# A chunked recurrence whose inputs come from the host with channels on the rows

## The chip, the cores and the metric

The kernel runs on one core of a Trainium2 chip. The metric is the device time of one execution in microseconds (us), the median of several runs. Five engines work side by side: TensorE (PE; PEld is its weight load), VectorE (DVE), ScalarE (ACT), GpSimd (POOL) and SyncE (SP, which here issues the DMAs). Each engine takes its own instructions strictly in order.

## The reference, cut to what matters

```python
def _attn_ref(r, k, v, w, a, b):                 # each (4, 8, 768, 40): batch, head, step, channel
    state = zeros((B, H, D, D))
    for t in range(S):
        y[:, :, t] = einsum('bhd,bhde->bhe', rt, state)
        Sa = einsum('bhde,bhe->bhd', state, at)
        state = state * wt[:, :, None, :] - einsum('bhd,bhe->bhde', Sa, bt) + einsum('bhd,bhe->bhde', vt, kt)
    return y

def reference(...):
    x = _attn_ref(r, k, v, w, a, b)              # then (4, 768, 320)
    x = _moe_ref(x, w_gate, wq, wk, wv, wo)      # causal attention of 4 experts, the best 2 per row weighted
    return _moe2_ref(x, w_in, w_spatial, b_spatial, w_out)   # relu(x w_in), norm, mixing over steps, w_out
```

The change touches only the inputs of `_attn_ref`; the two later stages are as they were.

## The kernel before, in words

The 768 steps of a batch are cut into chunks of C = 64. Inside a chunk the recurrence is solved as a triangular system, so that only one state of 40x40 per head goes from chunk to chunk. Two batches go together, and three chunks of both make a **unit**: 8 units in all (2 pairs of batches, 4 stretches of 192 steps). A unit has its 8 heads as 4 pairs, and a pair's 2x40 channels lie on 104 rows (40, a gap to row 64, 40).

**First phase** of a unit (`p1`), which needs no state. Per pair: `p_w` brings w with channels on the rows and makes running products forward (PP, L159) and back (RPE, L162 and L165); `p_kb` multiplies b and k by RPE (L171), `p_a` multiplies a by PP (ABD, L178) and sends it to WL by DMA (L180); `p_t` makes the products of kb with ABD on PE (L189), masked by DVE into WL (L193) and copied by ACT into the tiles TD and T21 (L196, L197); `p_kbt` transposes kb (L206, L207). Then, per unit: `p_l` transposes TD into L (L217, copy L218), `p_sub` inverts the 32-row triangles by 62 DVE instructions of which each needs the one before it (L227 and L229 in turn), and `p_xt` transposes the inverse (L237, copies L241).

The inputs lie in memory with steps as rows, so w, b, k and a of each pair come in as a slab of 96-step blocks (four DMAs of 30 KB, L134, six slab buffers) and are turned by four PE transposes (`tr`, L141) into a PSUM tile. b, k and a are read there by DVE; w is copied by ACT into W first (L157).

**Second phase** (`p2`, once per chunk, both batches in turn): `f_w` (L370, ACT copy L374), `f_st` (L380, L383), `amat(0)` (L316), `f_u1` (L387, L391, L393), `amat(1)` (L316, mask L322), `f_t21` (L397, L400), `ys` (L333), `f_u2` (L404, L407), `rr` (r transposed, L295, copy L296), `yk` (L341, L344, stored), `f_s` (new state, L416, then SV by DVE, L419 and L420) and `vt` (the solved rows and v of the chunk transposed together, L302, copy L304). `f_w` of the next chunk needs SV. `amat`, `ys` and `yk` belong to the chunk before.

**What sets the order.** PE's order is written out by hand: each chunk calls `pump` five times, and `pump` puts pieces of the first phase of later units there, by a list of (time, piece): the pairs' pieces of unit i + 2 over the 15 pumps of unit i, and `p_l`, `p_sub` and `p_xt` of unit i + 1 in the same unit i. So while unit 2 runs, DVE inverts the triangles of unit 3 and the pairs of unit 4 are made ready. Before unit 0 the whole first phase of unit 0 and the pairs of unit 1 run alone. The order on DVE, ACT, POOL and SP is fixed when the program is built, by the scheduler's own estimate of times.

Of the kernel before, what the change touches and what calls it, by code (L numbers as in the profile page):

```python
# [54 lines left out]

def recurrence(ctx, tc, r, k, v, w, a, b, ident, store_x, pre=None, tail=None):
    nc = tc.nc
    B, H, S, D = r.shape
    C = 64
# [29 lines left out]

    SLAB = [ap.tile([TS, SL, 2, 64], F32, name=f"slab{n}") for n in range(NSL)]  # L90
    RR = cp.tile([128, H, 64], F32, name="RR")
    WL = [home(i, 3).tile([128, H, UT], F32, name=f"WL{i}") for i in range(3)]
# [21 lines left out]
    nc.vector.memset(scan1[:, :, 0:1], 1.0)  # L114
    for t in SLAB:
        nc.vector.memset(t[:, :, :, D:], 1.0)
    nc.vector.memset(RR[:, :, D:], 1.0)
    for t in W65:
        nc.vector.memset(t, 0.0)
    for t in WL + VU + sum(SV, []):  # L120
        nc.gpsimd.memset(t, 0.0)

    src = {"w": w, "k": k, "b": b, "a": a}
    uses = []

    def load(n):
        if n >= len(uses):
            return
        nm, i, p = uses[n]
        bb, u = units[i]  # L130
        for q in range(BQ):
            for z in range(SL // BQ):
                t0 = u * CQ * C + z * TS
# [3 lines left out]
    def tr(nm, i, p):  # L137
        n = uses.index((nm, i, p))
        pt = ps.tile([128, SL, TS], F32, name="p1", bufs=P1B)
# [3 lines left out]
        return pt[:Q].rearrange("e s p -> e (s p)")  # L143

    def ct(x):
        return x.rearrange("e (c t) -> e c t", c=UC)

    def p1(i):
# [3 lines left out]
        def p_w(p):  # L152
            n = i * NP + p
            w65, rpe = W65[n % 2], RPE[n % 2]
# [76 lines left out]
        def p_xt(t0):  # L231
# [7 lines left out]
            for g in range(2):  # L239
# [10 lines left out]
        def spread(lst, g0, g1):  # L250
# [12 lines left out]

    def load_step(dst, of, g, q):
        if g >= nst:
            return
        i, c = divmod(g, CQ)
        bb, u = units[i]
        t0 = (u * CQ + c) * C
        nc.sync.dma_start(dst[:, :, :D], of[bb * BQ + q, :, t0:t0 + C, :].rearrange("h t d -> t h d"))  # L270

    def load_sv(g):
        for q in range(BQ):
            load_step(SV[q][g % 2][64:], v, g, q)

    def load_vu(g):
        for q in range(BQ):
            load_step(VU[q][64:], v, g, q)

    def load_r(g):  # L280
        for q in range(BQ):
            load_step(RR[64 * q:64 * q + 64], r, g, q)

    def y_items(g):
# [3 lines left out]
        s0 = [S0[q][g % 2] for q in range(BQ)]  # L288
        rt = [RT[g % RTB][:, :, q * C:(q + 1) * C] for q in range(BQ)]
        st = {}  # L290

        def rr():
            pr = ps.tile([128, NP, BQ * C], F32, name="p1", bufs=P1B)
# [3 lines left out]
            load_r(g + 1)  # L297

        def vt(q):
            pv = ps.tile([128, NP, 128], F32, name="y", bufs=YB)  # L300
            for p in range(NP):
                nc.tensor.transpose(pv[:, p], VU[q][:, 2 * p:2 * p + 2, :].rearrange("j h d -> j (h d)"), ident)  # L302
            st["vut", q] = wk.tile([Q, NP, 128], F32, name="vut")
            nc.scalar.copy(st["vut", q], pv[:Q])  # L304
            if q == BQ - 1:
                load_vu(g + 1)

        def amat(q):
# [3 lines left out]
            for p in range(NP):  # L312
                for j in range(2):
                    js = slice(j * 64, j * 64 + 64)
                    for h in range(2):
                        nc.tensor.matmul(pas[h][js, q, p], st["vut", q][HR[h], p, js], rt[q][HR[h], p],  # L316
                                         start=True, stop=True)
# [29 lines left out]

        return rr, vt, amat, ys, yk

    def p2(g, pump):  # L350
# [79 lines left out]

        _, _, amat, ys, yk = outs[-2] if len(outs) > 1 else (lambda *_: None,) * 5
        both(f_w)
# [22 lines left out]
    when = sorted([(x[0], i) + x[1:] for i in range(len(units)) for x in p1(i)], key=lambda x: x[0])  # L455
    uses += [(x[2], x[1], x[4]) for x in when if x[2] in "wkba"]
    for n in range(NSL):
        load(n)
    load_sv(0)
    load_vu(0)  # L460
    load_r(0)

# [8 lines left out]
    for i in range(len(units)):  # L471
# [4 lines left out]
        if last:  # L476
            _, _, amat, ys, yk = outs.pop()
            for f in (lambda: amat(0), lambda: amat(1), ys, yk):
# [7 lines left out]
        def pump():  # L486
            state["gap"] += 1
            gap = state["gap"]
            run_until(15 * i + gap)
            if state["raw"] and not any(x[2] in "wbka" for x in when):  # L490

# [15 lines left out]
        if state["prep"] is not None:  # L507
            for _ in state["prep"]:
                pass
    _, _, amat, ys, yk = outs[-1]  # L510
    for f in (lambda: amat(0), lambda: amat(1), ys, yk):
# [686 lines left out]
```

## Time and profile before

| | us |
|---|---|
| median of 3 runs | 1217.88 (1217.38 to 1218.54) |
| span of the profiled execution | 1222.0 |
| its start-up, up to the first `f_w` | 100.07 |
| one unit in the middle (unit 2) | 77.88 |
| units 0 to 7 | 100.07 to about 735 |
| the two later stages | about 735 to 1222 |

The profiled execution is 0.3% above the median. The profile's page gives the busy time of each engine over the span; the views by stretch give it for one stage, and the timeline of one engine gives its instructions in order, with the idle time before each and what ended it. Busy shares over the whole span mix stages in which different engines are late, so each stage is to be read by itself.

### The profile page before, as it was taken

The page shows a single profiled execution, that of the slowest core. Times are in us where ns is not written, and L with a number is a line of the kernel's source. Part 1 is how long each engine was busy: PE and PEld are TensorE (multiplying, and loading weights), DVE is VectorE, ACT ScalarE, POOL GpSimd, SP SyncE. Part 2 cuts the span into 40 slices and gives each one's busy share as a digit, 9 for nine tenths or more (in the row PEclk, how much of TensorE's full clock was granted, in tenths as well). Part 3 has the DMA queues.
Part 4 walks back from the last instruction along what each step waited for, and adds up shares of the span by engine and source line. Part 5 has one row for each costly group of instructions (what it writes and reads, how often), then busy time and mean ns, then how long its engine had stood idle before and what let it go on. Part 6 is the DMA issues. An engine that isn't in the chain of part 4 may idle for free.

```text
span 1222.0 us, 31926 instructions
## 1 busy us (share of the span) xinstructions
PE 1024.8 (84%) x12730; PEld 896.5 (73%) x12730; DVE 761.9 (62%) x1930; ACT 652.1 (53%) x1599; POOL 203.0 (17%) x381
## 2 busy tenths in 40 slices
PE   5757787787887969879797877798999899999998
PEld 3546676777776868768685665576898798789888
DVE  4586739467495474854835446988657656765650
ACT  2345564655645557465455445667555556555641
POOL 5011000010010100000002015802211211121131
PEclk9999767666766566676675766799999999989999
DMA  4333343333333333323211103210000001000000
GB/s 64 61 63 62 53 67 62 54 57 55 69 60 57 56 52 69 64 45 80 53 41 33 28 7 107 68 39 1 18 32 17 1 17 49 1 1 17 18 1 33
DMA packets 214663, 52.96 MB, mean 43 GB/s; under 512 B 204785, under 2 KB 210673, under 8 KB 214514
## 3 DMA queue, kind: packets, MB, share of 16 engines
q1 hardware_dynamic: 214514, 50.92, 21.2%
q8 instruction: 100, 1.64, 0.6%
q14 instruction: 49, 0.40, 0.1%
HBM read 39.07 MB, written 7.86 MB: 38 GB/s over the span
## 4 chain that ended last, share of the span: by engine, by line
PE 48%; DVE 28%; ACT 14%; issue 5%; DMA 3%; POOL 2%; SPq 1%; ACTq 0%; DVEq 0%; POOLq 0%
DVE X L229 5%; DVE sub L227 5%; PE mm L952 4%; PE mm L953 4%; PE mm L954 4%; ACT XTD L196 3%; ACT XTD L241 3%; PE p L141 2%; PE mp L911 2%; PE y L333 2%; PE mp L841 2%; PE pw L404 2%; PE y L341 2%; ACT f L881 2%; PE p L217 2%
## 5 line engine op out<-in xcount | busy, mean ns | idle before, releaser
L141 PE MATMUL p<-ident,slab 96*128 96x96 f32 x512 | 102.4, 340 | 43.7 <-ACT XTD L197 20.0
L141 PEld LDWEIGHTS p<-ident,slab 96*128 96x128 f32 x512 | 73.7, 194 | 60.7 <-ACT XTD L197 22.4
L227 DVE TENSOR_TENSOR sub<-L,X 96x31 f32<-96x31 f32 (+15 forms) x248 | 83.4, 336 | 17.0 <-ACT L L218 10.5
L196 ACT COPY XTD<-p 32x192 f32<-32x192 f32 x64 | 30.6, 479 | 110.4 <-DVE WL L193 109.9
L229 DVE TENSOR_TENSOR X<-X,sub 96x31 f32<-96x31 f32 (+15 forms) x248 | 83.1, 335 | 6.0
L881 ACT ACTIVATE f<-sc,nm 128x512 f32<-128x512 f32 (+2 forms) x110 | 59.4, 544 | 31.6 <-DVE nm L876 14.4
L602 DVE TENSOR_TENSOR ptl<-mp,pth 128x256 fp32r<-128x256 f32 (+2 forms) x126 | 57.0, 460 | 23.1 <-ACT pth L601 22.1
L876 DVE TENSOR_REDUCE nm<-sc 128x1 f32<-128x512 f32 (+2 forms) x110 | 54.6, 505 | 22.9 <-PE sc L874 18.6
L333 PE MATMUL y<-RT,S 40*40 40x64 f32 (+1 forms) x768 | 49.5, 308 | 22.4 <-DVE am L322 22.4
L159 DVE TENSOR_TENSOR_SCAN PP<-W,scan 104x390 f32<-104x390 f32 x32 | 30.9, 966 | 58.4 <-ACT W L157 58.4
L601 ACT CAST pth<-mp 128x256 fp32r<-128x256 f32 (+2 forms) x126 | 50.0, 409 | 32.3 <-PE mp L911 18.4
L202 POOL COPY PEN<-PP 40x6 f32<-40x6 f32 x64 | 25.7, 401 | 245.0 <-DVE PP L159 243.6
L333 PEld LDWEIGHTS y<-RT,S 40*40 40x40 f32 (+1 forms) x768 | 43.2, 194 | 25.6 <-DVE am L322 23.7
L193 DVE TENSOR_TENSOR WL<-p,mask 64x384 f32<-64x384 f32 x32 | 17.9, 560 | 67.6 <-PE xt L189 67.1
L316 PE MATMUL y<-RT,vut 40*64 40x64 f32 x1536 | 48.1, 259 | 12.2 <-ACT S L383 11.8
L911 PE MATMUL mp<-ident,f 128*128 128x128 f32 x294 | 51.5, 295 | 4.6 <-DVE f L897 2.3
L920 PE MATMUL pa<-pth,vv 128*128 128x256 f32 x168 | 47.5, 297 | 5.9 <-DVE at L932 3.8
L316 PEld LDWEIGHTS y<-RT,vut 40*64 40x64 f32 x1536 | 37.7, 164 | 19.0 <-ACT S L383 14.7
L952 PE MATMUL mm<-ws_h,vn_h 128*128 128x384 f32 x144 | 49.2, 341 | 0.4 <-ACT vn_h L601 0.3
L171 DVE TENSOR_TENSOR kb<-p,RPE 104x384 f32<-104x384 f32 x64 | 35.2, 554 | 22.4 <-PE p L141 20.9
L897 DVE TENSOR_SCALAR f<-f,sm 128x128 f32<-128x128 f32 (+2 forms) x96 | 45.3, 513 | 5.9 <-POOL sm L889 5.3
L953 PE MATMUL mm<-ws_l,vn_h 128*128 128x384 f32 x144 | 48.6, 338 | 0.0
(284 smaller groups left out, 3122.1 us busy)
## 6 DMA issues: line engine op xcount, KB each, us to landing
slab<-in_w_dram SPq DMA_DIRECT2D x128, 30.0 KB
slab<-in_b_dram SPq DMA_DIRECT2D x128, 30.0 KB
slab<-in_k_dram SPq DMA_DIRECT2D x128, 30.0 KB
slab<-in_a_dram SPq DMA_DIRECT2D x128, 30.0 KB
SV<-in_v_dram SPq DMA_DIRECT2D x48, 80.0 KB
VU<-in_v_dram SPq DMA_DIRECT2D x48, 80.0 KB
RR<-in_r_dram SPq DMA_DIRECT2D x48, 80.0 KB
WL<-ABD SPq DMA_DIRECT2D x64, 60.0 KB
```

The costliest lines, as they stand in the source:

```text
L141: nc.tensor.transpose(pt[:, s, :], SLAB[n % NSL][:, s].rearrange("p h d -> p (h d)"), ident[:TS, :TS])
L196: nc.scalar.copy(TD[:, :, g, n].rearrange("j t c -> j c t"), pt[gs, :, gs])
L227: nc.vector.tensor_mul(tv, L[:, j + 1:, j:j + 1].to_broadcast([96, n, m]), X[:, j:j + 1, :m].to_broadcast([96, n, m]))
L229: nc.vector.tensor_sub(X[:, j + 1:, :m], X[:, j + 1:, :m], tv)
L316: nc.tensor.matmul(pas[h][js, q, p], st["vut", q][HR[h], p, js], rt[q][HR[h], p], start=True, stop=True)
L333: nc.tensor.matmul(st["py"][q][hr.start:hr.start + m, p], s0[q][hr, p, :m], rt[q][hr, p], start=(p == 0), stop=False, skip_group_check=True)
L602: (lo_eng or nc.vector).tensor_sub(lo, src, hi.bitcast(F32))
L876: nc.vector.tensor_reduce(nm[:, z:z + 1], sc[:, :nn], op=OP.max, axis=AX.X, negate=True)
L881: nc.scalar.activation(pe[:, n0:n0 + nn], scs[z][:, :nn], AF.Exp, bias=nm[:, :1], accum_out=sm[:, z, i - i0:i - i0 + 1])
L911: nc.tensor.transpose(pp[:, j, z * 128:(z + 1) * 128], pes[z][:, (j0 + j) * 128:(j0 + j + 1) * 128], ident)
L952: nc.tensor.matmul(ps_, ah, bh, start=first, stop=False)
L953: nc.tensor.matmul(ps_, ah, bl_, start=False, stop=False)
```

## The change

All inputs of the recurrence are rearranged on the host, outside the timed program. For each unit and pair there is one array of 104 rows: first w with a zero ahead of each chunk and one column of padding at the end (391 columns), then b, k and a (1152 columns). It is loaded by two DMAs into one of three XIN buffers, and DVE reads w, b, k and a from there. r comes with channels on the rows (RT, two buffers), v comes both with steps on the rows and, in VT, with channels on the rows. The slabs, `tr`, `rr` and the copy of w are gone; `p_kb` is one instruction for b and k; `vt` transposes only the solved rows (64x64 in place of 128x128) and `amat` takes its other half from VT.

```diff
-    SLAB = [ap.tile([TS, SL, 2, 64], F32, name=f"slab{n}") for n in range(NSL)]
+    XIN = [ap.tile([Q, WX + 3 * UT], F32, name=f"xin{n}") for n in range(NSL)]
...
-        for q in range(BQ):
-            for z in range(SL // BQ):
-                nc.sync.dma_start(SLAB[n % NSL][:, q * SL // BQ + z, :, :D],
-                                  src[nm][bb * BQ + q, 2 * p:2 * p + 2, t0:t0 + TS, :].rearrange("h p d -> p h d"))
-        for s in range(SL):
-            nc.tensor.transpose(pt[:, s, :], SLAB[n % NSL][:, s].rearrange("p h d -> p (h d)"), ident[:TS, :TS])
-        load(n + NSL)
+        t = XIN[n % NSL]
+        for c0, c1 in ((0, WX), (WX, WX + 3 * UT)):
+            nc.sync.dma_start(t[:, c0:c1], x[bb, u, p, :, c0:c1])
...
-            pw = tr("w", i, p)
-            nc.scalar.copy(w65[:, :W].rearrange("e (c t) -> e c t", c=UC)[:, :, 1:], ct(pw))
+            w65 = slab(i, p)[:, :WX]
...
-            nc.vector.tensor_mul(st["kb", p][:, :, j], ct(tr("bk"[j], i, p)), st["ip", p])
+            kb = slab(i, p)[:, WX:WX + 2 * UT].rearrange("e (j c t) -> e j c t", j=2, c=UC)
+            nc.vector.tensor_mul(st["kb", p].rearrange("e c j t -> e j c t"), kb,
+                                 st["ip", p][:, None].to_broadcast([Q, 2, UC, C]))
...
-            pa = tr("a", i, p)
+            pa = slab(i, p)[:, WX + 2 * UT:]
             nc.vector.tensor_mul(ct(abd), ct(pa), PP[i % PPB][:, p, :, :C])
+            load(uses.index((i, p)) + NSL)
...
-        def rr():
-            for p in range(NP):
-                nc.tensor.transpose(pr[:, p], RR[:, 2 * p:2 * p + 2].rearrange("t h d -> t (h d)"), ident)
-            nc.scalar.copy(RT[g % RTB], pr[:Q])
+    def load_rv(g):
+            nc.sync.dma_start(RT[g % 2], rt_in[g])
+                nc.sync.dma_start(VT[q][g % 2], vt_in[g, q])
...
-                nc.tensor.transpose(pv[:, p], VU[q][:, 2 * p:2 * p + 2, :].rearrange("j h d -> j (h d)"), ident)
-            nc.scalar.copy(st["vut", q], pv[:Q])
+                nc.tensor.transpose(pv[:, p], VU[q][:C, 2 * p:2 * p + 2, :].rearrange("j h d -> j (h d)"), ident[:C, :C])
+            nc.scalar.copy(st["vut", q][0], pv[:Q])
```

The orders move too. On PE, at `p_l` in the first chunk of a unit, between `amat(0)` and `f_u1` (p1 is a PSUM tile, XTD holds TD), there stands before:

```order
L316 MATMUL y_2215<-RT0_98,vut_2163 64x64
L141 MATMUL p1_2232<-ident_60,slab0_83 128x96 x4
L217 MATMUL p1_2251<-ident_60,XTD_96 96x32 x16
L141 MATMUL p1_2269<-ident_60,slab1_84 128x96 x4
L217 MATMUL p1_2279<-ident_60,XTD_96 96x32 x16
L387 MATMUL pw_2181<-wsb0_2198,XTD_96 32x40
```

and now:

```order
L289 MATMUL y_1741<-RT0_94,ut_1689 64x64
L289 MATMUL y_1740<-RT0_94,VT00_96 64x64
L289 MATMUL y_1741<-RT0_94,VT00_96 64x64
L200 MATMUL p1_1767<-ident_60,XTD_92 96x32 x16
L200 MATMUL p1_1785<-ident_60,XTD_92 96x32 x16
L360 MATMUL pw_1707<-wsb0_1724,XTD_92 32x40
```

Nothing is put in the place of the two groups of four transposes, and both halves of L follow each other at once.

On DVE, at the end of the same unit's first chunk, where the new state is made in the middle of the inversion (sub and X are the inversion's tiles), there stands before:

```order
L227 TENSOR_TENSOR sub_2729<-L_2247,X_2248 96x255
L344 TENSOR_TENSOR xs_2539<-y_2389,PP0_99 104x256
L229 TENSOR_TENSOR X_2248<-X_2248,sub_2729 96x15x17
L227 TENSOR_TENSOR sub_2732<-L_2247,X_2248 96x252
L229 TENSOR_TENSOR X_2248<-X_2248,sub_2732 96x14x18
L419 TENSOR_TENSOR SV00_114<-pw_2543,SV01_115 40x8x40
L419 TENSOR_TENSOR SV10_116<-pw_2543,SV11_117 40x8x40
L227 TENSOR_TENSOR sub_2815<-L_2247,X_2248 96x247
L420 TENSOR_TENSOR SV00_114<-SV00_114,PEN1_104 40x8x40
```

and now:

```order
L140 SCALAR_TENSOR_TENSOR PP0_100<-xin1_84,scan1_82 104x390
L140 SCALAR_TENSOR_TENSOR PP0_100<-xin2_85,scan1_82 104x390
L140 SCALAR_TENSOR_TENSOR PP0_100<-xin0_83,scan1_82 104x390
L212 TENSOR_TENSOR X_1764<-X_1764,sub_2123 96x17x15
L143 RECIPROCAL RPE0_107<-PP0_100 104x6
L392 TENSOR_TENSOR SV00_113<-pw_2004,SV01_114 40x8x40
L392 TENSOR_TENSOR SV10_115<-pw_2004,SV11_116 40x8x40
L210 TENSOR_TENSOR sub_2126<-L_1763,X_1764 96x256
L146 SCALAR_TENSOR_TENSOR RPE0_107<-xin1_84,RPE0_107 104x390
L393 TENSOR_TENSOR SV00_113<-SV00_113,PEN1_105 40x8x40
L393 TENSOR_TENSOR SV10_115<-SV10_115,PEN1_105 40x8x40
```

L140 is the forward scan and L146 the backward one (the order prints scans so). Unit 1 runs here; PP0 is by now unit 4's. Three of unit 4's four forward scans stand in a row just ahead of the state (L392, L393), where two of the inversion's steps and one L344 stood. The fourth is the fifth instruction after the L146 above, behind both L393 and two of the inversion's steps: it reads xin1 too, so its w can be loaded only when that L146, the last reader of the w before, is done.

On ACT, in the second chunk of that unit, between `f_u1` and `p_xt` (T21 and TD lie in XTD, wsb is the right-hand side, the two tiles p1 and xt of `p_t` hold one head each), there stands before:

```order
L196 COPY XTD_96<-p1_2735 32x6x32 x2
L197 COPY XTD_96<-p1_2735 32x192
L196 COPY XTD_96<-xt_2736 32x6x32 x2
L197 COPY XTD_96<-xt_2736 32x192
L400 COPY wsb0_2630<-pw_2613 32x320
L400 COPY wsb1_2632<-pw_2613 32x320
L241 COPY XTD_96<-xt_2821 32x48x4 x8
```

and now:

```order
L179 COPY XTD_92<-p1_2168 32x6x32 x2
L180 COPY XTD_92<-p1_2168 32x192
L373 COPY wsb0_2079<-pw_2062 32x320
L373 COPY wsb1_2081<-pw_2062 32x320
L179 COPY XTD_92<-xt_2169 32x6x32 x2
L180 COPY XTD_92<-xt_2169 32x192
L224 COPY XTD_92<-xt_2251 32x48x4 x8
```

The two copies of `f_t21`'s result have moved between the heads, ahead of the copies that free the tile xt for `p_xt`.

## Rows read from the trace of the kernel before

**Rows 1.** Page, part 1: busy us, share of the span, instructions

```profile
PE 1024.8 (84%) x12730; PEld 896.5 (73%) x12730; DVE 761.9 (62%) x1930; ACT 652.1 (53%) x1599; POOL 203.0 (17%) x381
```

**Rows 2.** Stretches: length, busy PE, PEld, DVE, ACT, POOL (instructions); granted clock, DMA

```profile
0.00:100.07 100.07, 59.67 (x600) 44.12 (x601) 59.50 (x138) 38.46 (x85) 25.63 (x53) 1.00 0.38 63
...
251.62:329.50 77.88, 64.85 (x1245) 57.41 (x1245) 49.29 (x119) 43.73 (x101) 6.42 (x14) 0.65 0.34 59
562.00:626.80 64.80, 53.86 (x1090) 47.74 (x1092) 42.61 (x111) 30.31 (x67) 1.84 (x3) 0.64 0.32 66
...
735.00:1222.00 487.00, 441.34 (x2653) 394.75 (x2649) 318.09 (x850) 268.84 (x711) 123.04 (x209) 0.94 0.08 26
```

**Rows 3.** The same view for parts of unit 2 (its chunk 2 starts at 306.54)

```profile
251.62:261.32 9.70, 8.47 (x136) 7.27 (x138) 2.96 (x6) 5.53 (x13) 0.37 (x2) 0.72 0.38 59
261.32:295.80 34.48, 27.96 (x554) 24.66 (x548) 32.73 (x87) 12.76 (x30) 3.73 (x6) 0.60 0.34 58
298.00:306.54 8.54, 8.54 (x130) 7.79 (x131) 3.48 (x8) 7.47 (x16) 0.42 (x1) 0.67 0.31 50
306.54:329.50 22.96, 19.87 (x434) 17.65 (x433) 9.57 (x19) 15.86 (x38) 1.89 (x5) 0.70 0.38 71
264.00:272.00 8.00, 8.00 (x157) 7.13 (x156) 7.69 (x21) 1.32 (x3) 1.15 (x3) 0.50 0.30 54
```

**Rows 4.** PE's timeline in unit 2: start, length, [idle before <-what ended it]

```profile
281.71 1.44 PE L370 MATMUL pw<-SV,WL 128*64 128x40 f32 x32 [0.28 <-DVE SV L420]
...
298.00 0.87 PE L237 MATMUL xt<-ident,X 96*128 96x96 f32 x4 [4.23 <-ACT XTD L197]
...
300.65 1.11 PE L295 MATMUL p<-ident,RR 128*128 128x128 f32 x4
...
315.68 1.28 PE L397 MATMUL pw<-wsb,T 32*32 32x40 f32 x32 [2.31 <-ACT VU L393]
```

**Rows 5.** DVE's groups by line, 261.32 to 295.8: busy, mean ns, idle before

```profile
L227 DVE TENSOR_TENSOR sub<-L,X 96x31 f32<-96x31 f32 (+15 forms) x31 | 10.4, 336 | 1.7 <-ACT L L218 0.9
...
L159 DVE TENSOR_TENSOR_SCAN PP<-W,scan 104x390 f32<-104x390 f32 x2 | 1.9, 960 | 0.0
...
L171 DVE TENSOR_TENSOR kb<-p,RPE 104x384 f32<-104x384 f32 x3 | 1.6, 550 | 0.0
L193 DVE TENSOR_TENSOR WL<-p,mask 64x384 f32<-64x384 f32 x2 | 1.1, 560 | 0.1
...
L344 DVE TENSOR_TENSOR xs<-y,PP 104x256 f32<-104x256 f32 x2 | 0.8, 412 | 0.0
```

**Rows 6.** PE's groups by line, the whole of unit 2

```profile
L141 PE MATMUL p<-ident,slab 96*128 96x96 f32 x64 | 11.5, 328 | 3.3 <-ACT XTD L197 3.3
...
L295 PE MATMUL p<-ident,RR 128*128 128x128 f32 x12 | 3.3, 434 | 0.0
L302 PE MATMUL y<-ident,VU 128*128 128x128 f32 x24 | 3.3, 280 | 0.0
...
L380 PE MATMUL y<-ident,SV 72*128 72x72 f32 x24 | 2.4, 236 | 0.2 <-ACT vut L304 0.2
```

**Rows 7.** DVE's timeline: first and last step of two inversions, start-up and unit 0

```profile
54.30 0.20 DVE L227 TENSOR_TENSOR sub<-L,X 96x31 f32<-96x31 f32 x1 [0.31 <-ACT L L218]
...
94.47 0.19 DVE L229 TENSOR_TENSOR X<-X,sub 96x31 f32<-96x31 f32 x1
...
108.19 0.20 DVE L227 TENSOR_TENSOR sub<-L,X 96x31 f32<-96x31 f32 x1 [0.63 <-ACT L L218]
```

**Rows 8.** POOL's timeline and the chain of waits in the start-up; SP's timeline, unit 2

```profile
12.48 0.78 POOL L161 MEMSET RPE<- 104x384 f32 x2
...
16.91 2.55 DMA slab<-in_k_dram
...
263.25 2.45 SPq L134 DMA_DIRECT2D slab<-in_w_dram  x4
```

**Rows 9.** Stretches, as rows 2, after a burst of matmuls in unit 2

```profile
304.00:308.00 4.00, 3.97 (x92) 3.62 (x89) 3.14 (x7) 2.62 (x6) 0.00 (x0) 1.00 0.41 80
```

More of the change, by code (lines that the diff above doesn't have):

```diff
@@ L53, with recurrence @@
 PRW = 3
-def recurrence(ctx, tc, r, k, v, w, a, b, ident, store_x, pre=None, tail=None):
+def recurrence(ctx, tc, shape, x, rt_in, v_in, vt_in, ident, store_x, pre=None, tail=None):
     nc = tc.nc
-    B, H, S, D = r.shape
+    B, H, S, D = shape
     C = 64
@@ L114, in recurrence @@
     nc.vector.memset(scan1[:, :, 0:1], 1.0)
[L115 to L120, printed above, removed]
+    for t in VU + sum(SV, []) + WL:
         nc.gpsimd.memset(t, 0.0)
-    src = {"w": w, "k": k, "b": b, "a": a}
     uses = []
@@ L153, in p_w @@
             n = i * NP + p
[L154 removed]
+            rpe = RPE[n % 2]
             W = UC * (C + 1)
[L156 to L157 removed]
+            w65 = slab(i, p)[:, :WX]
             pp = PP[i % PPB][:, p]
@@ L262, in recurrence, with load_v @@
     nst = len(units) * CQ
[L264 to L270, printed above, removed]
+    def load_v(dst, g):
+        if g < nst:
+            for q in range(BQ):
+                nc.sync.dma_start(dst[q][64:], v_in[g, q])
     def load_sv(g):
-        for q in range(BQ):
-            load_step(SV[q][g % 2][64:], v, g, q)
+        load_v([SV[q][g % 2] for q in range(BQ)], g)
     def load_vu(g):
[L277 to L282, printed above, removed]
+        load_v(VU, g)
+    def load_rv(g):
+        if g < nst:
+            nc.sync.dma_start(RT[g % 2], rt_in[g])
+            for q in range(BQ):
+                nc.sync.dma_start(VT[q][g % 2], vt_in[g, q])
     def y_items(g):
@@ L346, in yk @@
                 store_x(bb * BQ + q, (u * CQ + c) * C, xs)
-        return rr, vt, amat, ys, yk
+        return vt, amat, ys, yk
     def p2(g, pump):
@@ L429, in p2 @@
         load_sv(g + 1)
-        _, _, amat, ys, yk = outs[-2] if len(outs) > 1 else (lambda *_: None,) * 5
+        _, amat, ys, yk = outs[-2] if len(outs) > 1 else (lambda *_: None,) * 4
         both(f_w)
@@ L455, in recurrence @@
     when = sorted([(x[0], i) + x[1:] for i in range(len(units)) for x in p1(i)], key=lambda x: x[0])
-    uses += [(x[2], x[1], x[4]) for x in when if x[2] in "wkba"]
+    uses += [(x[1], x[4]) for x in when if x[2] == "w"]
     for n in range(NSL):
@@ L460, in recurrence @@
     load_vu(0)
-    load_r(0)
+    load_rv(0)
+    load_rv(1)
     def run_until(gap):
@@ L476, in recurrence @@
         if last:
-            _, _, amat, ys, yk = outs.pop()
+            _, amat, ys, yk = outs.pop()
             for f in (lambda: amat(0), lambda: amat(1), ys, yk):
@@ L489, in pump @@
             run_until(15 * i + gap)
-            if state["raw"] and not any(x[2] in "wbka" for x in when):
+            if state["raw"] and not any(x[2] in "wba" for x in when):
                 state["raw"] = False
@@ L509, in recurrence @@
                 pass
-    _, _, amat, ys, yk = outs[-1]
+    _, amat, ys, yk = outs[-1]
     for f in (lambda: amat(0), lambda: amat(1), ys, yk):
@@ L1067, in blend, with kernel_body @@
             pos[n] += abs(x) / cost * (p1 - p0)
-def kernel_body(tc, r, k, v, w, a, b, w_gate, wq, wk, wv, wo, w_in, w_sp, b_sp, w_out, out):
+def kernel_body(tc, shape, x, rt, v, vt, w_gate, wq, wk, wv, wo, w_in, w_sp, b_sp, w_out, out):
     nc = tc.nc
-    B, H, S, D = r.shape
+    B, H, S, D = shape
     with ExitStack() as top:
@@ L1138, in kernel_body @@
         with ExitStack() as ctx:
-            recurrence(ctx, tc, r, k, v, w, a, b, ident, store_x, pre, tail)
+            recurrence(ctx, tc, shape, x, rt, v, vt, ident, store_x, pre, tail)
             parts["run"](None)
@@ L1169, in kernel_body, with layouts, rows, by_unit @@
                 stages[n].close()
-_INS = ["r", "k", "v", "w", "a", "b", "moe_w_gate", "moe_wq", "moe_wk", "moe_wv", "moe_wo", "moe2_w_in",
-        "moe2_w_spatial", "moe2_b_spatial", "moe2_w_out"]
+_INS = ["moe_w_gate", "moe_wq", "moe_wk", "moe_wv", "moe_wo", "moe2_w_in", "moe2_w_spatial", "moe2_b_spatial",
+        "moe2_w_out"]
 _OUTS = [((4, 768, 320), "float32")]
+def layouts(np, r, k, v, w, a, b):
+    B, H, S, D = r.shape
+    C, CQ, Q = 64, 3, 104
+    U = S // (CQ * C)
+    def rows(t, pad):
+        t = t.reshape(B // 2, 2, H // 2, 2, U, CQ, C, D).transpose(0, 4, 5, 2, 3, 7, 1, 6)
+        o = np.full(t.shape[:5] + (64,) + t.shape[6:], pad, t.dtype)
+        o[:, :, :, :, :, :D] = t
+        return o.reshape(t.shape[:4] + (128,) + t.shape[6:])[:, :, :, :, :Q]
+    def by_unit(t):
+        return t.transpose(0, 1, 3, 4, 5, 2, 6)
+    wt = by_unit(rows(w, 1.0))
+    wt = np.concatenate([np.zeros_like(wt[..., :1]), wt], -1).reshape(wt.shape[:4] + (-1,))
+    parts = [wt, np.zeros_like(wt[..., :1])] + [by_unit(rows(t, 0.0)).reshape(wt.shape[:4] + (-1,)) for t in (b, k, a)]
+    x = np.ascontiguousarray(np.concatenate(parts, -1))
+    n = S // C * (B // 2)
+    rt = np.ascontiguousarray(rows(r, 0.0).transpose(0, 1, 2, 4, 3, 5, 6).reshape(n, Q, H // 2, 2 * C))
+    vt = np.ascontiguousarray(rows(v, 0.0).transpose(0, 1, 2, 5, 4, 3, 6).reshape(n, 2, Q, H // 2, C))
+    vs = v.reshape(B // 2, 2, H, S // C, C, D).transpose(0, 3, 1, 4, 2, 5).reshape(n, 2, C, H, D)
+    vp = np.zeros((n, 2, C, H, 64), v.dtype)
+    vp[..., :D] = vs
+    return {"x": x, "rt": rt, "v": vp, "vt": vt}
 def kernel(**inputs):
@@ L1183 @@
     arrays, args = {}, []
-    for name in _INS:
-        a = _np.ascontiguousarray(inputs[name])
+    given = layouts(_np, *(_np.asarray(inputs[n]) for n in "rkvwab"))
+    given.update((n, _np.ascontiguousarray(inputs[n])) for n in _INS)
+    for name, a in given.items():
         if a.dtype == _np.float64:
@@ L1193 @@
     with tile.TileContext(nc, schedule_with_timeline_sim=True) as tc:
-        kernel_body(tc, *args)
+        kernel_body(tc, inputs["r"].shape, *args)
     r = _run(nc, [arrays], core_ids=[0])
```

46 lines of the change are left out of this document (18 added, 28 removed).

## The prediction

> **What bounds the kernel now.** The page's totals come first: PE is busy for 84% of the span and DVE for 62% [rows 1]. Read alone, this says that PE binds and that whatever leaves PE is gained. The view by stretches corrects it. The two later stages (487.0 us) have no instruction of the change; I hold them fixed. The start-up (100.07 us) has PE busy for 59.67 and DVE for 59.50, so there the engines wait for each other. A middle unit takes 77.88 us with PE busy for 64.85 [rows 2].
>
> Cutting unit 2 shows three regimes [rows 3]. From 261.32, where the inversion of the next unit's triangles begins, to 295.80 DVE works 32.73 of 34.48 us, while PE works 27.96. The groups by line say on what: 31 pairs of dependent steps, L227 at 336 ns and L229 alike, 20.8 us, and around them masks, scans and products [rows 5]. What PE does less in this stretch saves nothing. PE waits there: L237 starts at 298.00 after 4.23 us of idle time that the copies to T21 ended [rows 4]. From 298.00 to 306.54 PE is busy throughout, but ACT is busy for 7.47 of these 8.54 us. From 306.54 to 329.50, chunk 2, DVE is busy for 9.57 only and PE for 19.87 of 22.96 [rows 3]; here PE's work counts, apart from the 2.31 us in which it waits for ACT [rows 4].
>
> **The change part by part.** All sums stand against the profiled span of 1222.0 us, 0.3% above the median of 1217.88; the last step carries this over.
>
> *PE's side.* Per unit 64 transposes of the slabs go, 11.5 us busy, and 12 of r, 3.3 us. The 24 of `vt` shrink from 128 to 64 columns; their nearest row is L380 at 72 columns, 236 against 280 ns, so 24 x 0.044 = 1.1 us. That is 15.9 of 64.85 us [rows 2, 6]. A group of four slab transposes is 11.5 / 16 = 0.72 us.
>
> *Chunk 0 up to the inversion.* Two such groups go from between `amat` and L, on the path to the first L227: 9.70 us become 9.70 - 1.4 = 8.3 [rows 3, 6].
>
> *The DVE-bound stretch.* What leaves PE here counts at nothing, since DVE covers it. DVE's own content is changed by the order. Before, it holds two forward and two back scans (0.96 each), three products L171 (0.55) and two L178 like them [rows 5]; L178 is a product of L171's shape and I price it so. After, it holds four forward scans, two back scans, one product of doubled width and one for ABD: the unit's scans no longer wait for a transpose and a copy by ACT, and have been moved forward into this stretch. The doubled product costs between one old one (0.55) and two (1.10); by the slope between L344 (256 columns, 412 ns) and L171 (384 columns, 550) it is 0.55 + 3 x 0.138 = 0.96, which I take [rows 5]. So +2 x 0.96 - 3 x 0.55 + 0.96 - 0.55 = +0.7 us, of which I count +0.5, since neighbours overlap by about a tenth.
>
> One wait is new: the fourth forward scan. Its w (104 x 391, 163 KB) can be asked for only when the back scan before it is done; between them stand two L393 and two steps of the inversion, about 1.9 us. A 30 KB slab landed 2.55 us after its issue [rows 8], which is the lower bound; the upper one adds 163 KB at the 59 GB/s that the unit's transfers ran at [rows 2]: 2.8 more, 5.3 us. I take the nearer row, 2.55, hence +0.65, because 59 GB/s is what was asked for and not a measured limit. All of DVE's queue stands behind this scan, and PE behind DVE.
>
> On the way to `p_xt` ACT now does the two copies of `f_t21`'s result ahead of the second head's copies, 0.8 us later for L237; the group of slab transposes between L237 and `f_u2` (0.7) goes. Chunk 0 and the start of chunk 1 come to -1.4 + 0.5 + 0.65 + 0.8 - 0.7 = -0.15 us: nothing.
>
> *298.00 to 306.54.* PE loses `rr` (1.1) and two slab groups (1.4) [rows 4, 6], but `f_u2`'s result is copied by ACT behind eight copies of the inverse, and `f_s` waits for that. ACT's 7.47 us [rows 3] cover what PE loses: between -0.3 and -2.5, and I take -0.3.
>
> *Chunk 2.* `rr` goes (-1.1), and one group of L206 moves to chunk 1 (about -0.6): -1.7. The wait of `f_t21` for ACT stays. `vt` counts at nothing: it stands in the shadow of SV on DVE.
>
> A middle unit gains 0.15 + 0.3 + 1.7 = 2.1 us; **units 1 to 5: -11**. *Unit 6* has 53.86 of 64.80 us on PE [rows 2] and no inputs left to prepare: three `rr`, -3. *Unit 7*: -2, its gaps being filled with pieces of the next stage.
>
> *Start-up and unit 0.* Before, 40 of 100 us pass with DVE idle [rows 2]; its inversion starts at 54.30 and ends at 94.47 [rows 7]. After, DVE has before that end, by its order, 15 forward scans, 12 back scans, 10 double products, 10 ABD, 16 masks and the 62 steps: 14.4 + 11.5 + 9.6 + 5.5 + 9.0 + 20.8 = 70.8, by starts about 66 [rows 5]. It can run densely only from about 13, when POOL has cleared RPE behind the larger tiles [rows 8]. With four waits of 2.5 us for reloaded buffers the inversion ends at 13 + 66 + 10 = 89, 5.5 earlier. The next inversion began at 108.19 [rows 7]; two groups (1.4) and the scan pair ahead of it go too: about -8. Unit 0 itself then has none of its four forward scans left on DVE (-3.8), and chunk 2 gives -1.7. **Together -13**, between -3 and -20.
>
> The sum is -13 - 11 - 3 - 2 = -29: span 1193, and with the 0.3% **1189 us**.
>
> **The rivals.** *A, all of PE's work counts.* 15.9 us in each of units 0 to 5 and 3.3 to 4 in the last two make -103, and the start-up gives -20: 1222 - 123 = 1099, median 1095. For it speaks PE's 84% [rows 1]; against it the stretch in which DVE works 32.73 of 34.48 us [rows 3]. A milder form, in which ACT does not cover 298 to 306, gives 2.2 x 6 = 13 more than my sum: 1176.
>
> *B, a slower PE.* From 264 to 272, transposes and narrow matmuls, PE was busy throughout at a granted clock of 0.50, the lower level of 1.2 GHz [rows 3]; after a burst of L341 and L416 it was granted 1.00, 2.4 GHz, from 304 to 308 [rows 9]. If PE idles more beside DVE, chunk 2 (clock 0.70 on average) may start and stay at the lower level. At 0.50 its 19.87 us of work become at most 19.87 x 0.70 / 0.50 = 27.8; narrow matmuls do not scale so (L380 and L302 differ by a sixth for nearly double the columns [rows 6]), so I price a third of it, 2.5 us in six units: +15, span 1208, **1204**. The Trainium skill, "TensorE: Matmul & The Clock Gate", Part 1, says that the throttled clock is the default and that activity releases it, which speaks against a change that takes work off PE. The same page's Part 4 says that transposes do not count as PE-busy in the same way; by that rule the removed ones gave no clock, and B falls. No row parts the two.
>
> *C, slower: w lands late.* The fourth forward scan waits in each of units 1 to 5, and in the start-up some seven more of that kind stand before reloaded buffers. SP issues strictly in order, and a 480 KB part (b, k, a) is in flight ahead of w. At 5.3 us instead of 2.55 the cost is 12 x 2.75 = 33: 1193 + 33 = 1226, **1222**. The point from which it decides is 2.55 + 29 / 12 = 5.0 us from issue to landing. For it speaks 59 GB/s in units [rows 2]; against it, that SP spent 2.45 us on four issues of one slab of short rows [rows 8], which limited the rate by itself. The Trainium skill, "DMA: Bandwidth & Descriptors", Specifications, puts line rate at 512 bytes per transfer or more; the new rows have 1.5 KB and 4.6 KB, the old ones 160 bytes. By that the landing is near the lower bound; no row here shows it.
>
> *D, no change.* The scans' new place costs all that the start-up gains: within 2.4 us of 1218.
>
> **How the numbers follow.** Chances: my forecast with the milder form 0.63, A 0.05, B 0.17, C 0.10, D 0.05. About 0.2%, 2.4 us, can be told from no change. Forecast and B hold 0.80: from 1168 (the milder form with a start-up of -20 in place of -13: 1176 - 7 = 1169) to 1209 (B with a start-up some 5 worse). Faster: 0.63 + 0.05 + 0.17 and a little of C, 0.86; same 0.06; slower 0.08.
>
> **What would show it.** Right: the first inversion ends near 89 and the next begins near 100; a middle unit takes about 76 us; the stretch from the first step of the inversion to the second mask keeps its 34 to 36 us with DVE over 90% busy; chunk 2 takes about 21. Wrong by A: units of 62 us and a stretch in which DVE idles. Wrong by B: chunk 2 at a clock below 0.6 and not shorter than 22.96. Wrong by C: forward scans that wait over 2.5 us for xin, in each unit. My start-up term is the least sure: it rests on an order and on waits that no row shows.

## The result: 1.4% slower

The changed kernel takes 1235.29 us (median of 4 runs) against 1218.21 beside it: ratio 1.014, interval 1.0121 to 1.0159. The forecast was 1189, the range ended at 1209. The profiled executions are 1231.4 and 1222.0 us long; the stages below are those of the profiles, so they add up to 9.4 of the 17 us (the profile of before happens to lie above its median, that of after below).

| us | before | after | change | forecast |
|---|---|---|---|---|
| start-up, to the first `f_w` | 100.1 | 104.4 | +4.3 | -5.5 |
| unit 0 | 74.2 | 70.5 | -3.7 | -7.5 |
| units 1 to 5 | 387.3 | 396.0 | +8.7 | -11 |
| unit 6 | 65.2 | 68.6 | +3.4 | -3 |
| unit 7 and the later stages | 595.2 | 591.9 | -3.3 | -2 |

The page and the stretches of after that answer to [rows 1 to 3], in the same columns (the granted clock is the third number from the end of a line). The stretches are the start-up, unit 2, in it the first step of the inversion to the second mask, the end of chunk 1 and chunk 2, and unit 6:

```profile
PE 968.3 (79%) x12122; PEld 852.3 (69%) x12122; DVE 757.3 (61%) x1889; ACT 615.8 (50%) x1543; POOL 195.0 (16%) x381
...
0.00:104.40 104.40, 29.93 (x473) 24.42 (x473) 69.39 (x140) 33.39 (x75) 30.70 (x62) 1.00 0.43 111
...
255.57:335.59 80.02, 60.77 (x1168) 53.73 (x1169) 49.19 (x115) 38.42 (x91) 4.89 (x14) 0.53 0.31 81
264.17:300.87 36.70, 25.16 (x518) 22.25 (x512) 34.00 (x86) 11.36 (x28) 0.42 (x1) 0.50 0.22 61
303.65:312.53 8.88, 7.52 (x114) 6.49 (x115) 4.24 (x9) 6.39 (x14) 0.42 (x1) 0.50 0.42 108
312.53:335.59 23.06, 20.62 (x416) 18.32 (x417) 9.22 (x18) 12.74 (x30) 1.52 (x3) 0.55 0.39 98
570.94:639.54 68.60, 55.68 (x1081) 50.03 (x1082) 42.80 (x112) 28.82 (x69) 1.84 (x3) 0.56 0.33 88
```

Three things are to be seen. PE's work in the start-up is halved (59.67 to 29.93 us), yet the start-up is longer. The DVE-bound stretch is 36.70 us in place of 34.48. And in chunk 2 PE has less to do but is busy longer, 20.62 against 19.87 us, at a granted clock of 0.55 against 0.70 [rows 3].

The 1.00 that the column gives for the start-up, here and in [rows 2], can't be read as full speed. It stands for unit 0 of the changed kernel too (70.5 us), yet there `f_w`'s matmuls (L343) take 309 ns and L353's transposes 334, as in unit 4 at 0.50 to 0.56 (309 and 336); and the fourth experiment below, whose column gives 0.53 for the same unit, needs 70.4 us for it. A mean over the whole span counts these stretches in, so clocks are compared below from unit 1 on. No term of the prediction rests on it.

DVE's groups in the start-up, and two instructions of its timeline there, show whom the scans wait for:

```profile
L140 DVE TENSOR_TENSOR_SCAN PP<-xin,scan 104x390 f32<-104x390 f32 x15 | 14.3, 967 | 23.6 <-DMA xin<-in_x_dram 23.6
...
56.65 0.97 DVE L146 TENSOR_TENSOR_SCAN RPE<-xin,RPE 104x390 f32<-104x390 f32 x1 [0.34 <-POOL RPE L142]
60.91 0.97 DVE L140 TENSOR_TENSOR_SCAN PP<-xin,scan 104x390 f32<-104x390 f32 x1 [3.30 <-DMA xin<-in_x_dram]
```

The back scan L146 frees a buffer at 57.6, SP, busy until 58.0 with the transfers of ABD to WL, issues the load of w at 58.11, and the forward scan, next in DVE's queue, stands until 60.91.

### The profile page after: what moved, and what is told of

It reads as the page before. It is cut to its first block, busy times and chain, and to the rows that moved or that the text cites. A ratio compares the mean times of both kernels' runs of the same rounds, so it can differ in the third digit from the quotient of the medians.

```text
span 1231.4 us, 29699 instructions
## 1 busy us (share of the span) xinstructions
PE 968.3 (79%) x12122; PEld 852.3 (69%) x12122; DVE 757.3 (61%) x1889; ACT 615.8 (50%) x1543; POOL 195.0 (16%) x381
## 2 busy tenths in 40 slices
DMA packets 55714, 68.60 MB, mean 56 GB/s; under 512 B 25561, under 2 KB 39769, under 8 KB 55578
## 4 chain that ended last, share of the span: by engine, by line
PE 42%; DVE 29%; ACT 16%; issue 6%; DMA 4%; POOL 3%; SPq 1%; DVEq 0%; ACTq 0%; POOLq 0%
DVE sub L210 6%; DVE X L212 5%; ACT XTD L224 4%; PE mm L927 4%; PE mm L928 4%; PE mm L929 4%; DMA xin<-in_x_dram 3%; ACT XTD L179 3%; PE mp L886 2%; PE y L306 2%; PE mp L816 2%; PE y L289 2%; DVE PP L140 2%; DVE am L295 2%; DVE WL L176 2%
## 5 line engine op out<-in xcount | busy, mean ns | idle before, releaser
L172 PE MATMUL p<-ABD,kb 40*64 40x64 f32 x768 | 53.6, 314 | 29.2 <-DVE kb L152 15.7
L172 PEld LDWEIGHTS p<-ABD,kb 40*64 40x64 f32 x768 | 47.6, 219 | 31.7 <-DVE kb L152 15.7
L343 PE MATMUL pw<-SV,WL 128*64 128x40 f32 x768 | 47.7, 289 | 25.8 <-DVE SV L393 11.8
L172 PE MATMUL xt<-ABD,kb 40*64 40x64 f32 x768 | 50.5, 313 | 21.4 <-ACT XTD L180 18.6
L306 PE MATMUL y<-RT,S 40*64 40x64 f32 (+1 forms) x768 | 52.9, 314 | 17.4 <-DVE am L295 17.4
L343 PEld LDWEIGHTS pw<-SV,WL 128*64 128x64 f32 x768 | 43.2, 203 | 32.1 <-issue 18.4
L289 PE MATMUL y<-RT,ut 40*64 40x64 f32 x768 | 60.2, 310 | 6.3 <-ACT S L356 5.5
L172 PEld LDWEIGHTS xt<-ABD,kb 40*64 40x64 f32 x768 | 45.7, 220 | 22.5 <-ACT XTD L180 19.5
L306 PEld LDWEIGHTS y<-RT,S 40*64 40x64 f32 (+1 forms) x768 | 45.7, 197 | 21.8 <-DVE am L295 19.1
L289 PEld LDWEIGHTS y<-RT,ut 40*64 40x64 f32 x768 | 48.6, 209 | 14.3 <-ACT S L356 6.6
L289 PE MATMUL y<-RT,VT 40*64 40x64 f32 x768 | 51.6, 310 | 0.0
```

The lines of the kernel that those rows point to most:

```text
L172: nc.tensor.matmul(pts[h][j * 64:j * 64 + 64, c], kb[HR[h], c, j], abd[HR[h], c * C:(c + 1) * C], start=True, stop=True)
L289: nc.tensor.matmul(pas[h][js, q, p], st["vut", q][j][HR[h], p], rt[q][HR[h], p], start=True, stop=True)
L306: nc.tensor.matmul(st["py"][q][hr.start:hr.start + m, p], s0[q][hr, p, :m], rt[q][hr, p], start=(p == 0), stop=False, skip_group_check=True)
L343: nc.tensor.matmul(pw[q][:, h], WL[par][:, h, cq[q] * C:(cq[q] + 1) * C], sv[q][:, h, :D], start=(h == 0), stop=False, skip_group_check=True)
```

## The experiments

Theory 1: the forward scans, which wait for nothing on PE any more, were moved ahead by the scheduler, into the DVE-bound stretch and up against their loads. Theory 2: PE, with less to do, is granted the lower clock (0.50) for more of the time and gives the gain back. Against both stands that the loads themselves, or PE's work alone, set the time.

**Six buffers.** `NSL = 3` became `NSL = 6`.

> The changed kernel with six XIN buffers in place of three, nothing else. Theory: in the start-up the forward scans, moved ahead, use up the three buffers, so that each next scan waits for a load that could be issued only when a back scan just before it was done; DVE waits 27 us there for loads of w. Then with six buffers these waits nearly vanish, the first f_w comes at 93 to 97 us in place of 104.4, and the whole takes some 8 to 11 us less, about 1226. Rival (the start-up is bound by POOL, PE and the dependence of the pairs, the waits for loads only hide this): first f_w at 102 to 105, whole time within 3 us of the changed kernel's 1235. The middle units stay at 80 us by both.

1234.75 us, first f_w at 108.5. DVE's wait in the start-up stays:

```profile
L140 DVE TENSOR_TENSOR_SCAN PP<-xin,scan 104x390 f32<-104x390 f32 x16 | 15.3, 967 | 28.3 <-DMA xin<-in_x_dram 28.2
```

The theory of too few buffers falls; the rival's total came, its 102 to 105 for the first f_w did not. Now 16 forward scans stand before the first f_w; the fourth to sixth wait 2.0, 2.4 and 2.3 us for loads that were asked for at the very start, and later ones, up to 4.1 us, again behind a back scan.

**Scans held.**

```diff
-            nc.vector.tensor_tensor_scan(pp..., w65..., scan1...)
+            with tc.issue_after(marks["v"]) if "v" in marks else ExitStack():
+                nc.vector.tensor_tensor_scan(pp..., w65..., scan1...)
```

> The changed kernel with each forward scan held, on DVE's queue, behind the last state update (L393) that the program wrote before it. By its order each chunk then has its scans, reciprocal, product and back scan right behind the state, and the stretch of the inversion keeps one forward and one back scan in place of four and two. Theory (the scans that the scheduler moved ahead cost the units their gain): first step of the inversion to second mask 32 to 33 us in place of 36.7, a middle unit 76 to 77 us in place of 80.0, whole time 1212 to 1220. Rival (the units are slow because PE works at the lower clock): the stretch shrinks but chunk 2 and the end of chunk 1 stay at 23.1 and 8.9 us or grow, a unit 78 us or more, whole time 1224 or more.

1207.34 us, ratio 0.9908 (0.9874 to 0.9943): faster than before, and below the theory's range. Start-up, unit 2 and its stretch from the first step of the inversion to the second mask, chunk 2:

```profile
0.00:91.72 91.72, 29.78 (x473) 24.38 (x473) 63.41 (x131) 33.35 (x75) 29.92 (x58) 1.00 0.49 123
238.10:313.60 75.50, 59.15 (x1169) 52.34 (x1170) 48.71 (x115) 38.51 (x92) 12.85 (x14) 0.57 0.34 87
246.72:279.12 32.40, 25.24 (x518) 22.29 (x514) 30.39 (x81) 11.01 (x27) 4.32 (x3) 0.50 0.41 103
290.70:313.60 22.90, 20.50 (x417) 18.20 (x418) 9.29 (x18) 12.64 (x30) 2.13 (x5) 0.55 0.33 81
```

With the same work the start-up loses 12.7 us and unit 2 loses 4.5, 4.3 of them in the stretch. Five forward scans of later units have left the start-up (10 in place of 15), and DVE's wait for xin there falls from 23.6 to 12.7 us. Theory 1 is shown, and chunk 2 stands as it did: what keeps it there is something else. Held scans have a price as well: in every kernel that has them chunk 2 of unit 3 takes 24.7 to 27.3 us (22.6 in the changed kernel); why was not tried.

**Dummy transposes and dense matmuls.** The third experiment puts four transposes of the identity (`idle()`) where each group of slab transposes and `rr` stood; the fourth puts eight dense matmuls (`warm(8)`) ahead of `p_xt(0)`.

> The changed kernel with dummy transposes of the identity where the slabs' and r's transposes stood (64 and 12 per unit, as large as those, results read by nobody). Theory of the clock (PE's removed work had kept it up): granted clock in a middle unit back from 0.53 to about 0.65, chunk 2 no longer than 23.0 us although PE has some 2 us more to do in it, whole time 1225 to 1235. Rival (PE's work counts and the clock does not): units 3 to 4 us longer than the changed kernel's 80.0, whole time 1250 to 1260.

> The changed kernel with eight dense matmuls (128x128 by 512 columns, bf16, read by nobody) ahead of the first transposes of the inverse in chunk 1, where PE sits idle for 4.9 us. Theory of the clock: granted clock near 1.00 behind them, the rest of chunk 1 and chunk 2 together 31.9 us now take 28 to 29, the whole 12 to 18 us less, about 1220. Rival (what follows is bound by ACT's copies and the dependences): 31 to 32 us as before, whole time 1233 to 1238.

1240.55 and 1238.23 us: neither forecast of the clock's theory held for the whole; the fourth's total stands at the upper end of the rival's. The third raised unit 2 to a clock of 0.56 only (from 0.53). Unit 2 costs 1.6 us more, units 1 to 5 on average 0.5, well under the rival's 3 to 4. But it shows the price of the clock within one kernel, in chunk 2 of units 2 and 4, same instructions:

```profile
314.39:338.09 23.70, 23.13 (x433) 20.37 (x433) 9.22 (x18) 13.14 (x32) 1.52 (x3) 0.57 0.40 104
...
475.28:497.30 22.02, 18.90 (x432) 16.48 (x433) 9.22 (x18) 12.70 (x30) 1.52 (x3) 0.77 0.32 84
```

0.20 of clock are 4.2 us of PE's busy time and 1.7 us of the chunk. In the fourth the clock rose to 0.93 from 302 to 306 of unit 2 and was at 0.50 from 306 to the end of chunk 2 (23.6 us): what the dense matmuls gave was gone before the chunk began.

**One part alone.** r and v from the host with the old slabs, and the other way round.

> The kernel before with r and v alone laid out by the host (no transposes of r, those of v halved); w, b, k, a still come as slabs and are turned on PE. In chunk 2 of a unit PE is never behind DVE. Theory of the prediction's step (what leaves PE there counts): chunk 2 about 21.7 us in place of 22.9, a middle unit 1.4 us shorter than the kernel before, units 6 and 7 two to three each, whole time 1202 to 1208. Rival (PE loses the clock or the wait moves to ACT's copies): chunk 2 stays at 22.5 to 23.5, units within 1 us of before, whole time 1214 to 1222.

> The changed kernel with r and v as in the kernel before (transposed on PE), w, b, k, a from the host. Theory (the scans that the scheduler moved ahead are the loss, and they come with this part alone): first f_w at 103 to 106 us, inversion's first step to second mask 36 to 38 us, whole time 1232 to 1248. Rival (r's and v's loads on SP's queue, or the lower clock after the loss of their transposes, are a good part of the loss): 1218 to 1226.

1216.83 us, ratio 0.9985 (0.9958 to 1.0012), and 1215.55, ratio 0.9963 (0.9942 to 0.9984). The fifth gave both theories half: chunk 2 of units 2 and 3 took 21.8 and 21.3 us (forecast 21.7), but that of unit 4 23.9 at a clock of 0.53, and unit 6 gained 0.3 us, not 3; the total is the rival's. In the sixth the scans cost what they cost in the changed kernel: first f_w at 102.8, and the inversion of unit 2 from 258.74 to 295.60. Its second mask falls ahead of the last steps here, at 292.76 to 293.31, so the inversion is measured by its own steps:

```profile
292.76 0.55 DVE L177 TENSOR_TENSOR WL<-xt,mask 64x384 f32<-64x384 f32 x1
...
295.41 0.19 DVE L213 TENSOR_TENSOR X<-X,sub 96x31 f32<-96x31 f32 x1
```

That is 36.9 us, against 36.1 in the changed kernel, 33.4 before and 31.3 with held scans. Yet the whole takes 20 us less than the changed kernel, a little under the rival's 1218 to 1226: theory 1 holds in its place and is not the whole. So r's and v's part, which by itself changes nothing that can be told, costs 20 us on top of the other. Unit 6, which has no w, b, k, a to prepare, differs between the sixth and the changed kernel by that part alone:

```profile
555.05:619.28 64.23, 53.53 (x1093) 47.49 (x1094) 42.37 (x112) 31.87 (x70) 1.84 (x3) 0.65 0.31 66
```

64.23 at 0.65 against 68.60 at 0.56, with 12 more PE instructions (1093 and 1081). But the fifth's unit 6, which has as little for PE as the changed kernel's (1080 instructions), takes only 64.9 us at 0.60: what runs before a unit counts as well. Over units 1 to 5 the clock is 0.67 before, 0.59 in the fifth, 0.61 in the sixth and 0.54 in the changed kernel.

**Dense matmuls with the scans held; the transposes of the inverse freed.** Two dense matmuls where each group of four stood; and, in `p_xt`, `nm = "p1"`.

> The changed kernel with the forward scans held as in the second experiment, and two dense matmuls (128x128 by 512 columns, bf16, read by nobody) where each group of four transposes stood in the kernel before. Theory (the clock takes the gain of chunk 2 and of the end of chunk 1): granted clock in a middle unit 0.75 or more in place of 0.57, chunk 2 at 20 to 21.5 us, a unit 73 to 74.5 in place of 75.4, whole time 1190 to 1203. Rival (what PE does there counts for itself, whatever the clock): a unit of 77 us or more, whole time 1213 or more.

> The second experiment's kernel with the first transposes of the inverse (L220) written to a tile of the larger PSUM pool in place of the one tile that the products of the second head's mask also use, so that they wait for the last step of the inversion alone. Theory (between the second mask and these transposes stand ACT's copies, 3.1 us): L220 at +40.5 to +41.5 us of a unit in place of +44.1, chunk 1 shorter by 1 to 2.5 us, whole time 1196 to 1203. Rival (ACT's queue binds what follows anyway, the copies only move): chunk 1 within 0.5 us, whole time 1205 to 1210.

1210.89 us: chunk 2 of units 1, 2, 4 and 5 came to 21.2 to 21.9 us at 0.76 to 0.77, near what the clock's theory has, but the filling cost chunk 0 of unit 2 5.7 us (30.9 against 25.2). That unit takes 77.2 us at 0.60, the rival's length, and the whole lies between the two forecasts. 1205.61 us: the transposes came at +40.0, four us earlier, and chunk 1 lost 0.5 us: ACT's queue binds what follows, the rival is right.

**Held scans with r and v on PE.** The sixth kernel with its scans held as in the second; then with five buffers; then also with `nm = "p1"`.

> The sixth experiment's kernel (w, b, k, a from the host, r and v transposed on PE as before) with the forward scans held as in the second. Theory (two causes that add up: the scans moved ahead cost the start-up and the units, and the lost transposes of r and v cost PE its higher clock): first f_w at 90 to 93 us, a middle unit 72 to 74.5 us, unit 6 at 64 to 65.5, whole time 1186 to 1197. Rival (the second experiment has already all that can be had, the clock follows DVE's pace): a unit 75 to 77, whole time 1203 to 1210.

> As the ninth, with five XIN buffers in place of three. Theory (with the scans held, loads come early enough for the start-up's 16 us of waits on DVE to go): first f_w some 3 to 6 us earlier than the ninth's, whole time 3 to 6 us less. Rival (five buffers ask for more data at the start and delay the rest, as six did in the first experiment): first f_w 2 to 5 us later.

> As the tenth, with the first transposes of the inverse in the larger PSUM pool as in the eighth. Expected 2 us less than the tenth (the eighth was 2 less than the second), the units 0.3 us shorter.

1184.57 us, ratio 0.9725 (0.9709 to 0.9742), first f_w at 89.4, unit 2 at 74.0, unit 6 at 63.4: the theory of two causes, the whole and unit 6 even a little under its ranges. With five buffers 1194.45, first f_w 2.5 us later: the rival there; the rest of the loss of 10 (5 us in units 4 and 5, 2 behind unit 6) is not explained. The eleventh, 1196.31, gained nothing.

**Which work kept the clock.** The changed kernel with one edit (its tile and copy changed to match):

```diff
-                nc.tensor.transpose(pv[:, p], VU[q][:C, ...], ident[:C, :C])
+                nc.tensor.transpose(pv[:, p], VU[q][:, ...], ident)
```

> The changed kernel with the transposes of the solved rows at their old full size (128 rows into 128 columns, of which only the first half is copied), nothing else. Theory (of what the change took from PE, this work at the end of each chunk, just before the next f_w, is what kept the higher clock): unit 6 back from 68.6 to 64 to 66 us, chunk 2 of a middle unit at a clock over 0.6, whole time 1215 to 1225. Rival (the transposes of r, in the middle of the chunk, or the sum of all kept it): unit 6 at 68 or more, whole time 1233 to 1240.

1208.67 us, ratio 0.9919 (0.9901 to 0.9937): 24 transposes of each unit made twice as wide, and the kernel is 27 us faster, more than forecast. Its units 1 to 6 together, chunk 2 of unit 2, unit 6, and, of unit 4, two of PE's groups that the edit does not touch:

```profile
173.80:617.58 443.78, 339.52 (x6889) 302.28 (x6890) 275.56 (x662) 222.88 (x528) 24.64 (x71) 0.60 0.30 79
306.73:328.19 21.46, 18.33 (x418) 16.32 (x417) 8.95 (x18) 12.90 (x31) 1.52 (x3) 0.64 0.40 106
...
555.07:617.58 62.51, 50.56 (x1082) 45.28 (x1082) 42.33 (x112) 28.39 (x67) 1.83 (x3) 0.65 0.36 95
...
L343 PE MATMUL pw<-SV,WL 128*64 128x40 f32 x96 | 4.8, 256 | 3.5 <-DVE SV L393 2.9 <-PE y L275 0.5
...
L353 PE MATMUL y<-ident,SV 72*128 72x72 f32 x24 | 2.9, 269 | 2.5 <-ACT ut L277 2.5
```

and units 1 to 6 and the same groups of unit 4 in the changed kernel:

```profile
174.91:639.54 464.63, 357.61 (x6889) 317.20 (x6890) 276.68 (x662) 223.17 (x528) 24.09 (x71) 0.54 0.29 76
...
L343 PE MATMUL pw<-SV,WL 128*64 128x40 f32 x96 | 6.5, 309 | 4.5 <-issue 3.6 <-PE y L275 0.9
L353 PE MATMUL y<-ident,SV 72*128 72x72 f32 x24 | 3.9, 336 | 1.1 <-ACT ut L277 1.1
```

With more to do PE is busy 18 us less; the untouched instructions are 17 and 20% shorter. First f_w comes at 105.7, so nothing of the gain is the start-up's. DVE's order differs in places from the changed kernel's, but not in unit 2: there DVE, ACT and POOL have the same instructions in the same order, and the unit is 3.0 us shorter all the same. Its chunk 1, at 0.50 and 0.51, takes 28.8 and 29.2 us; its chunk 0 goes from 28.2 us at 0.55 to 26.4 at 0.68, and chunk 2 from 23.1 at 0.55 to 21.5 at 0.64. Theory 2 is shown for this work.

**Useless work at that place, and both cures.** Four transposes of the identity at the end of each chunk of the changed kernel; and the twelfth kernel with its scans held.

> The changed kernel with four dummy transposes of the identity (128x128, read by nobody) at the end of each chunk, behind the transposes of the solved rows and ahead of the next f_w: work that is added and takes nothing out. Theory (work at this place keeps the higher clock): unit 6 at 63 to 66 us in place of 68.6, chunk 2 of a middle unit at a clock over 0.6 and no longer than 22.5, whole time 1208 to 1225, less than the changed kernel's 1235 although PE has more to do. Rival (the full-size transposes of the twelfth experiment are faster for another reason, their form or their operand of 128 rows): unit 6 at 68 or more, whole time 1235 to 1250.

> The twelfth experiment's kernel (full-size transposes of the solved rows, r from the host) with the forward scans held as in the second. Theory (two causes, each with its own place: they add): 1235 less 28 for the scans less 27 for the clock, 1176 to 1188, first f_w at 90 to 93, unit 6 at 62 to 64. Rival (held scans leave PE busier, so that the clock's part is had twice): 1195 to 1206. Against the ninth (1184.6, r transposed on PE) it tells whether the transposes of r are worth more off PE or on it.

1240.99 us: the total is the rival's. Unit 6 is the theory's, 64.80 us against 68.60 with work only added, though its mean clock is hardly higher (0.58 against 0.56; in its chunk 2 0.64 against 0.50):

```profile
574.86:639.66 64.80, 54.78 (x1093) 48.94 (x1094) 42.26 (x111) 26.65 (x63) 1.83 (x3) 0.58 0.32 88
```

In units 1 to 5 chunk 2 came to 23.6 to 25.5 us at 0.55 to 0.71, a miss for the theory. There the dummy takes a tile of the pool that the transposes of kb need, and these wait 1.7 to 2.5 us for ACT in units 1 to 3; whether that is all of it was not tried. So the twelfth shows that the full-size transposes bring back part of the clock (0.60 over units 1 to 6; 0.54 in the changed kernel, 0.66 before), and whether other added work would do the same is left open.

1179.33 us, ratio 0.9678 (0.9664 to 0.9693). 1235.3 - 27.9 (second) - 26.6 (twelfth) = 1180.8: the two causes add. It is the fastest kernel here, and 5 us under the ninth, so r's transposes are better off PE.

## Why the prediction was wrong, step by step

**The edit's gain is there.** With both causes taken away it is 1218.5 - 1179.3 = 39 us, more than the 29 forecast. Two causes took 56. How much of the 39 us belongs to the held scans themselves is not known: they were not tried on the kernel before, and its inversion, 33.4 us, was longer than the held 31.3.

**The start-up (forecast -5.5, measured +4.3)** failed in one number: "four waits of 2.5 us". DVE stood 23.6 us for w, 21.6 of them behind 12.94 us in nine waits of 2.4 us each. The price was right, the count was not: every forward scan moved ahead stands behind the back scan that frees its buffer. So the first inversion ended at 103.0 where 89 was forecast, and 11.6 of these 14 us are waits. With the scans held, and 12.7 us of waits, it ended at 90.3 and the first f_w comes at 91.7; I had 94.6. The order that I quoted ahead of the prediction had this pattern in it; I followed it through the middle unit and not through the start-up.

**Chunk 0 and the DVE-bound stretch.** The first step came at 8.60 us of the unit (forecast 8.3). The stretch grew by 2.2 us, forecast 0.5 + 0.65. The wait for w was 0.77; DVE's busy time grew by 1.27, not 0.5. The sign was right; that the scans could be held back against the scheduler's order, and what its order cost against that (4.3 us), I did not ask. Between the second mask and the transposes of the inverse 0.6 us were added (forecast 0.8).

**End of chunk 1, chunk 2, unit 6 (forecast -1.0 with the slab group, -1.7, -3; measured +0.3, +0.1, +3.4).** The step that failed took PE's durations from rows at one clock and let the clock stay: it priced what leaves PE at -1.7 us of chunk 2, and the clock there fell from 0.70 to 0.55, so that PE was busy 20.62 us in place of 19.87. Rival B had the mechanism, at 2.5 us in six units, and both of its signs came (a clock under 0.6, and not under 22.96 us). By the twelfth run it is worth 2.3 to 3.3 us in each of units 0 to 5, 6 in unit 6 and 3 behind it, so its size was right for a unit and short for the whole. B's chance of 0.17 was also put as an alternative to the forecast, where it could add to a bad start-up.

**Rival C** named the waits on loads but blamed the landing. It had seven in the start-up, where 11 of the 15 scans waited, and from 48 to 96 us five loads of w took 2.4 to 3.9 us from issue to use, mostly over the 2.55 of the forecast and all under the 5.0 from which C decides. In unit 2 the wait was 0.77 us, not over 2.5. **Rival A** is refuted: PE's busy time fell by 56 us in the page and the time rose.

**The Trainium skill**, "TensorE: Matmul & The Clock Gate", Part 1, says that the clock is throttled by default and released by activity. The twelfth run agrees (0.56 to 0.65 in unit 6, 0.54 to 0.60 over units 1 to 6). Part 4 of the page says that transposes do not count as PE-busy in the same way; here the clock rose with transposes that were only made wider, and units 1 to 5 of the third experiment, with nothing but idle transposes added, had 0.59 in place of 0.54. The measurement decides: in this kernel they count for something.

What stays open is why the time does not follow the clock: either part alone lowers it over units 1 to 5 (0.67 to 0.59 and 0.61) and these units are still 5 and 3 us shorter, both together bring it to 0.54 and they are 9 us longer. Open is also why five buffers cost the later units.

## What to carry to other kernels

Work taken off an engine can free an instruction from the wait that kept it in place; look where the scheduler then puts it, through every stage, and hold it if it lands ahead of a dependent chain or of its own load. More buffers did not cure that here. If PE runs near its lower clock, do not price removed PE work by the old durations: price the rest at both levels, and try whether cheap work, left in place, keeps the clock up; work that was added afresh did not pay here (1240.6 and 1241.0 us).

## What was not expected of the hardware

That a kernel became 27 us faster (1235.3 to 1208.7) when 24 transposes of each unit were made twice as wide, at a granted clock of 0.60 in place of 0.54 over units 1 to 6; and that idle transposes alone shortened unit 6 from 68.60 to 64.80 us, while they lengthened the whole by 5.7 us.
